# A six-layer cross network on one core: the first 512 rows of the input enter as plain rows and are transposed on TensorE, and the first remainder weights enter as 32 rows

## The chip, the core and the metric

The kernel runs on one core of a Trainium2 chip. A core has TensorE (PE in the profile, with its weight loads shown as PEld), VectorE (DVE), ScalarE (ACT), GpSimd (POOL) and SyncE (SP), and 16 DMA engines that all queues share. The metric is the device time of one launch in microseconds (us). Before the change the median of three runs is 131.31 us (131.15 to 131.46).

## The reference

```python
x = x0                                   # 4096 x 416, bf16
for l in range(6):
    x = x0 * (x @ ws[l] + bs[l]) + x     # ws: 6 x 416 x 416, bs: 6 x 416
```

Six cross layers follow each other. Each multiplies all 4096 rows by a 416 x 416 matrix, adds a bias, multiplies by the original input and adds the layer's input.

## The kernel before, in words

For layers 0 to 4 the activations are kept transposed: the 416 features lie on partitions, the 4096 batch rows on the free axis. 416 is three blocks of 128 features and a remainder of 32. The three blocks are the tile `XM[i]` (128 partitions x 3 x 4096); `XM[0]` holds x0, and two more take the layers' outputs in turn. The batch is cut into two halves `s` of four groups `g` of 512 columns. The 32 remainder features of a half's four groups are stacked on 128 partitions in `XR[i]` (group g on partitions 32g to 32g+31). `XRd` is a copy of x0's remainder with its upper and lower 64 partitions exchanged.

**Loads (lines 100 to 121).** `load_x0t(s, g)` (L76) issues a transposing DMA on SP: 512 rows x 384 columns of x0 arrive as three 128 x 512 blocks of `XM[0]`. All eight are on SP's queue, in the order (0,0), (0,1), (0,2), (0,3), (1,0), then `load_xrem1` (L85), then (1,1) to (1,3). Behind them on SP are the weights of layers 1 to 5, x0 as plain rows for the last layer, and its bias. ACT's queue issues layer 0's weights `WM[:,0]` (L72), the biases `bsb` (L102), four loads `xrig` (L81, the remainder columns of half 0 in 64-byte pieces), and `WR[:,0]` (L88): the 32 remainder rows of layer 0's weights, read four times so that they stand on all four 32-partition groups. A planner gives each DMA one of eight completion semaphores in turn, and an issue that reuses a semaphore first waits for that semaphore's earlier DMA: the WR load waits, on ACT, for the first transposing load.

**TensorE's head.** Two fillers of 256 columns and eight of 512 (L135) run on a constant tile. Then `bias_setup` transposes the biases (L143, L145; VectorE copies them, L146 and L147), and a ninth 512-column filler goes where the planner's order puts it.

**`first_layer(s)`** is the part that the change touches. A PSUM tile `ph` holds 128 output features (block m) x two groups (a pair h), and four such tiles fit in PSUM. For half 0 it goes so:

1. `full(m, 0, 0)` for m = 0, 1, 2: three matmuls each (L206, k = 0, 1, 2) on group 0, nine in all;
2. `x0_rem(0)` (L151): four TensorE transposes of `xrig` into `tpr`, then three VectorE copies (L154), one into `XR[0]` and two of 64 partitions into `XRd`;
3. `full(m, 0, 1)`: nine matmuls on group 1;
4. the row stage (`row`, L213): eight matmuls of 32 rows with `WR`, for pair 0 of each block and for pair 1 of block 0. Those on different 32-row groups of the array run side by side;
5. ScalarE evicts each `ph` with the bias (L159), VectorE multiplies by x0 (L160) and adds the input (L161);
6. pair 1: 18 matmuls L206, four row matmuls, 16 of the remainder outputs (L185, L190) into `pr`, and `x0_rem(1)` for half 1 into the other half of `pr`; ScalarE's eviction of `pr` is L165.

Half 1 is the same without step 2. Layers 1 to 4 (L173, L179) then run on TensorE back to back, and the last layer (L319, L325, L346, L347, L336) writes rows out. `WD` (L125) is a block-diagonal copy of 32 columns of `WR` that GpSimd makes.

The order of instructions on each engine comes from the tile planner; `tc.keep_in_program_order` pins a single instruction to its place in the program.

Of the kernel before, what the change touches and what calls it, by code (L numbers as in the profile page):

```python
# [10 lines left out]
ALU = mybir.AluOpType  # L11
BF16 = mybir.dt.bfloat16
FP32 = mybir.dt.float32
# [3 lines left out]
def kernel(  # L17
# [7 lines left out]
    nc = tc.nc  # L25
    B, D = x0.shape
    L = ws.shape[0]
    P = 128
    NK = 3
    R = D - NK * P  # L30
    assert R == 32 and B == 4096 and D == 416 and L >= 2
    NS = 2
    NG = 4
    CW = 512
# [5 lines left out]
    big = ctx.enter_context(tc.tile_pool(name="big", bufs=1))  # L40
    tpool = ctx.enter_context(tc.tile_pool(name="tpool", bufs=6))
    opool = ctx.enter_context(tc.tile_pool(name="opool", bufs=10))
    psum = ctx.enter_context(tc.tile_pool(name="psum", bufs=4, space=bass.MemoryType.PSUM))

    x0_v = x0.rearrange("(bt p) d -> p bt d", p=P)
    out_v = out.rearrange("(bt p) d -> p bt d", p=P)

    ident = const.tile([P, P], BF16)
    dz = const.tile([P, 2], FP32)
    warm = const.tile([P, CW], BF16)  # L50
    ones = const.tile([P, P], BF16)
    WM = const.tile([P, L, NK, D], BF16)
    WR = const.tile([P, L, D], BF16)
# [3 lines left out]
    bM = const.tile([P, NK, L], FP32)  # L57
    bR = const.tile([P, L], FP32)
    X0rows = big.tile([P, NBT, D], BF16)
    XLrows = big.tile([P, NBT, D], BF16)  # L60
    scrR = [big.tile([P, 4, P], BF16, name=f"scrR{s}") for s in range(NS)]
    xrem = big.tile([P, 16, R], BF16)
    xrig = big.tile([P, NS, 4, P], BF16)
    XRd = big.tile([P, NS * CW], BF16)
    XM = [big.tile([P, NK, B], BF16, name=f"XM{i}") for i in range(3)]
    XR = [big.tile([P, NS * CW], BF16, name=f"XR{i}") for i in range(3)]

    def col0(s, g):
        return SW * s + CW * g

    def load_wm(eng, l):
        eng.dma_start(WM[:, l], ws[l, 0:NK * P, :].rearrange("(k p) n -> p k n", p=P))  # L72

    def load_x0t(s, g):
        c0 = col0(s, g)
        nc.sync.dma_start_transpose(out=XM[0][:, :, c0:c0 + CW], in_=x0[c0:c0 + CW, 0:NK * P])  # L76

    def load_xrem0():
        with nc.allow_non_contiguous_dma(reason="64B row segments"):
            for i in range(4):  # L80
                nc.scalar.dma_start(xrig[:, 0, i, :].rearrange("p (g r) -> p g r", g=NG), x0_v[:, i:16:4, NK * P:D])  # L81

    def load_xrem1():
        with nc.allow_non_contiguous_dma(reason="64B row segments"):
            nc.sync.dma_start(xrem[:], x0_v[:, 16:32, NK * P:D])  # L85

    def load_wr0():
        nc.scalar.dma_start(WR[:, 0, :], ws[0:1, NK * P:D, :].broadcast_to([NG, R, D]))  # L88

    def load_wr(eng, g, l0, l1):  # L90
        eng.dma_start(WR[32 * g:32 * g + 32, l0:l1, :], ws[l0:l1, NK * P:D, :].rearrange("l r n -> r l n"))
# [5 lines left out]
    nc.gpsimd.memset(ones[:], 1.0)  # L97
    nc.gpsimd.memset(WD[:], 0.0)

    load_x0t(0, 0)  # L100
    load_wm(nc.scalar, 0)
    nc.scalar.dma_start(bsb[:], bs[:, :])  # L102
    load_x0t(0, 1)
    load_xrem0()
    load_wr0()
    nc.scalar.activation(dz[:, 1:2], dz[:, 0:1], ACT.Identity, bias=dz[:, 0:1], scale=1.0)  # L106
    for g in range(2, NG):
        load_x0t(0, g)
    load_x0t(1, 0)
# [18 lines left out]
    nc.gpsimd.tensor_copy(xrig[:, 1].rearrange("p i (g r) -> p i g r", g=NG), xrem[:].rearrange("p (g i) r -> p i g r", g=NG))  # L128
    fill_wd(1, L)

    wps = psum.tile([P, CW], FP32, tag="ps", name="wps")

    def pe_filler(n, cols):
        for i in range(n):
            nc.tensor.matmul(wps[:, 0:cols], lhsT=warm[:, 0:P], rhs=warm[:, 0:cols], start=True, stop=True)  # L135

    pe_filler(2, 2 * P)
    pe_filler(8, CW)

    def bias_setup():  # L140
        pb = psum.tile([P, 4, 8], BF16, tag="ps", name="pb")
        for m in range(NK):
            nc.tensor.transpose(pb[:, m, 0:L], bsb[0:L, 128 * m:128 * m + 128], ident[0:L, 0:L])  # L143
        for g in range(NG):
            nc.tensor.transpose(pb[32 * g:32 * g + 32, 3, 0:L], bsb[0:L, NK * P:D], ident[0:L, 0:L], tile_position=(0, 32 * g))  # L145
        nc.vector.tensor_copy(bM[:], pb[:, 0:NK, 0:L])  # L146
        nc.vector.tensor_copy(bR[:], pb[:, 3, 0:L])  # L147

    def x0_rem(s, tpr):
        for i in range(4):  # L150
            nc.tensor.transpose(tpr[:, 128 * i:128 * i + 128], xrig[:, s, i, :], ident[:])  # L151
        for dst, src in ((slice(0, P), slice(0, P)), (slice(64, P), slice(0, 64)), (slice(0, 64), slice(64, P))):
            to = XR[0] if dst == src else XRd
            nc.vector.tensor_copy(to[dst, CW * s:CW * s + CW], tpr[src])  # L154

    def ew_main(l, s, m, h, pt, cur, nxt):
        c0 = col0(s, 2 * h)
        t = tpool.tile([P, 2 * CW], BF16, name="t")
        nc.scalar.activation(t[:], pt[:].rearrange("p a b -> p (a b)"), ACT.Identity, bias=bM[:, m, l:l + 1], scale=1.0)  # L159
        nc.vector.tensor_tensor(out=t[:], in0=t[:], in1=XM[0][:, m, c0:c0 + 2 * CW], op=ALU.mult)  # L160
        nc.vector.tensor_tensor(out=nxt[:, m, c0:c0 + 2 * CW], in0=t[:], in1=cur[:, m, c0:c0 + 2 * CW], op=ALU.add)  # L161

    def ew_rem(l, s, pr, curR, nxtR):
        tr = tpool.tile([P, 2 * CW], BF16, name="t")
        nc.scalar.activation(tr[:, 0:CW], pr, ACT.Identity, bias=bR[:, l:l + 1], scale=1.0)  # L165
        nc.vector.tensor_tensor(out=tr[:, 0:CW], in0=tr[:, 0:CW], in1=XR[0][:, CW * s:CW * s + CW], op=ALU.mult)  # L166
        nc.vector.tensor_tensor(out=nxtR[:, CW * s:CW * s + CW], in0=tr[:, 0:CW], in1=curR[:, CW * s:CW * s + CW], op=ALU.add)  # L167
# [15 lines left out]
    def mm_rem(l, s, pr, cur, curR):  # L183
        for g in range(NG):
            nc.tensor.matmul(pr[32 * g:32 * g + 32, :], lhsT=WD[:, l, g, :], rhs=curR[:, CW * s:CW * s + CW],  # L185
                             start=True, stop=False, tile_position=(0, 32 * g))
        for k in range(NK):
            for g in range(NG):
                c0 = col0(s, g)
                nc.tensor.matmul(pr[32 * g:32 * g + 32, :], lhsT=WM[:, l, k, NK * P:D], rhs=cur[:, k, c0:c0 + CW],  # L190
                      start=False, stop=(k == NK - 1), tile_position=(0, 32 * g))
# [8 lines left out]
    def first_layer(s):  # L200
        cur, curR, nxt, nxtR = XM[0], XR[0], XM[1], XR[1]

        def full(pt, m, h, gl, after_row):
            c0 = col0(s, 2 * h + gl)
            for k in range(NK):
                nc.tensor.matmul(pt[:, gl, :], lhsT=WM[:, 0, k, 128 * m:128 * m + 128], rhs=cur[:, k, c0:c0 + CW],  # L206
                                 start=(k == 0 and not after_row), stop=(k == NK - 1 and after_row))

        def row(pt, m, h, opens):
            for gl in range(2):  # L210
                rg = 32 * ((2 * h + gl) ^ (2 if m == 1 else 0))
                src = XRd if m == 1 else curR
                nc.tensor.matmul(pt[:, gl, :], lhsT=WR[rg:rg + 32, 0, 128 * m:128 * m + 128],  # L213
                                 rhs=src[rg:rg + 32, CW * s:CW * s + CW],
                                 start=opens, stop=not opens, tile_position=(rg, 0))

        def ph(m):
            return psum.tile([P, 2, CW], FP32, tag="ps", name=f"ph{m}")

        pa = [ph(m) for m in range(NK)]  # L220
        if s == 0:
            for m in range(NK):
                full(pa[m], m, 0, 0, False)
            tp0 = psum.tile([P, CW], BF16, tag="ps", name="tpr")
            x0_rem(0, tp0[:])
            for m in range(NK):
                full(pa[m], m, 0, 1, False)
        else:
            for m in range(NK):
                for gl in range(2):  # L230
                    full(pa[m], m, 0, gl, False)
        pb = [ph(0)]
        row(pa[0], 0, 0, False)
        row(pb[0], 0, 1, True)
        row(pa[2], 2, 0, False)
        row(pa[1], 1, 0, False)
        for m in range(NK):
            ew_main(0, s, m, 0, pa[m], cur, nxt)
        for m in range(NK):
            if m:  # L240
                pb.append(ph(m))
            for gl in range(2):
                full(pb[m], m, 1, gl, m == 0)
        row(pb[1], 1, 1, False)
        row(pb[2], 2, 1, False)
        pr = psum.tile([P, 2, CW], FP32, tag="ps", name="pr")
        mm_rem(0, s, pr[:, 0, :], cur, curR)
        if s == 0:
            x0_rem(1, pr[:, 1, :].bitcast(BF16)[:, 0:CW])
        for m in range(NK):  # L250
            ew_main(0, s, m, 1, pb[m], cur, nxt)
        ew_rem(0, s, pr[:, 0, :], curR, nxtR)

    bias_setup()
    pe_filler(1, CW)
    for s in range(NS):
        first_layer(s)

# [14 lines left out]
    cur, curR = XM[1], XR[1]  # L273
    for l in range(1, LL):
        nxt, nxtR = XM[1 + (l % 2)], XR[1 + (l % 2)]
# [4 lines left out]
        def finish(t):  # L280
            s, m = t
            for h in range(2):
                ew_main(l, s, m, h, pts[t][h], cur, nxt)
            if feeds_last:
                xl_dmat(s, m, nxt)
# [19 lines left out]
        cur, curR = nxt, nxtR  # L305

    l = LL
# [97 lines left out]
```

## Time and profile before

| what | value |
|---|---|
| median of 3 runs | 131.31 us (131.15 to 131.46) |
| the profiled execution, its own time | 131.51 us |
| its span, first to last instruction | 129.7 us |
| TensorE busy | 123.4 us, 95% of the span |
| VectorE busy | 107.5 us, 83% |
| ScalarE busy | 85.7 us, 66% |
| GpSimd busy | 6.1 us, 5% |
| mean granted TensorE clock | 0.992 |

The span is 1.8 us shorter than the execution's own time; that part lies outside the instructions. In the lists of groups a row gives busy time and the mean duration of one; a matmul's shown duration overlaps the next one's, so TensorE's pace is read from the starts. The chain view follows the work that ended last back to what released it. In the timeline the first number is the start and the second the length of the merged piece, both in us.

### The profile page before, as it was taken

Reading aid. Unit: us, or ns where it says so; the run is one execution under the profiler, and the core shown is the slowest. Engines: PE = TensorE matmul, PEld = TensorE weight load, DVE = VectorE, ACT = ScalarE, POOL = GpSimd, SP = SyncE. Lnnn points to the kernel's source line nnn. Section 1 sums busy time; section 2 is a strip of 40 time slices with the busy share of each in tenths; the row PEclk is TensorE's granted clock in tenths of the full one; section 3 lists DMA queues with packets and bytes.
Section 4 is the critical chain, followed back from the end, with each engine's and each line's share of the span. In section 5 each row is a group of like instructions: output and inputs, shape, how many; then the busy total and the mean of one; then the engine's idle time right before and its main releaser. Section 6 shows DMA issues by size and latency. Waiting matters only on the chain.

```text
span 129.7 us, 3968 instructions
## 1 busy us (share of the span) xinstructions
PE 123.4 (95%) x1690; PEld 55.1 (42%) x1690; DVE 107.5 (83%) x197; ACT 85.7 (66%) x97; POOL 6.1 (5%) x17
## 2 busy tenths in 40 slices
PE   6999999999999999999999999999999999999960
PEld 2333343444444444444444444444444445445430
DVE  1022999999998898999898989898989899888992
ACT  0044865976849486849476849577848896569670
POOL 4002200800000000000000000000000000000000
PEclk9999999999999999999999999999999999999996
DMA  3999999999990000000000000000197989996754
GB/s 91 240 222 226 167 163 269 257 329 333 332 274 7 0 5 3 5 0 5 0 5 0 5 0 5 0 0 5 26 180 163 121 180 199 187 315 195 237 182 137
DMA packets 42185, 16.45 MB, mean 127 GB/s; under 512 B 30894, under 2 KB 42168, under 8 KB 42168
## 3 DMA queue, kind: packets, MB, share of 16 engines
q1 hardware_dynamic: 39368, 15.53, 54.3%
q10 hardware_dynamic: 2800, 0.67, 2.6%
q8 instruction: 13, 0.21, 0.7%
q14 instruction: 4, 0.03, 0.1%
HBM read 6.23 MB, written 3.41 MB: 74 GB/s over the span
## 4 chain that ended last, share of the span: by engine, by line
PE 73%; DVE 11%; DMA 8%; issue 3%; ACT 2%; DVEq 0%; ACTq 0%
PE pt L173 49%; PE py L319 8%; PE pt L179 5%; PE pr L190 4%; DMA WR<-in_ws_dram 4%; DMA XM<-in_x_dram 4%; DVE t L347 3%; PE ph L206 3%; DVE t L160 2%; DVE XM L161 2%; DVE o L336 2%; PE pr L185 2%; PE ph L213 1%; PE py L325 1%; ACT t L159 1%
## 5 line engine op out<-in xcount | busy, mean ns | idle before, releaser
L173 PE MATMUL pt<-XM,WM 128*32 128x512 bf16 x1152 | 65.2, 379 | 0.0
L159 ACT ACTIVATE t<-pt,bM 128x1024 bf16<-128x1024 f32 x48 | 49.6, 1115 | 18.3 <-PE pt L179 18.3
L160 DVE TENSOR_TENSOR t<-t,XM 128x1024 bf16<-128x1024 bf16 x60 | 41.4, 690 | 6.0 <-ACT t L159 6.0
L161 DVE TENSOR_TENSOR XM<-t,XM 128x1024 bf16<-128x1024 bf16 x60 | 41.8, 697 | 3.5
L173 PEld LDWEIGHTS <-WM 128*32 128x32 bf16 x1152 | 29.7, 97 | 33.8 <-issue 5.1
L346 ACT CAST t<-py 128x416 bf16<-128x416 f32 (+1 forms) x23 | 14.8, 642 | 4.8 <-PE py L319 2.1
L319 PE MATMUL py<-WM,XM 128*128 128x416 bf16 x96 | 17.7, 340 | 0.0
L206 PE MATMUL ph<-XM,WM 128*128 128x512 bf16 x72 | 16.5, 379 | 0.2 <-DMA XM<-in_x_dram 0.2
L159 ACT ACTIVATE t<-ph,bM 128x1024 bf16<-128x1024 f32 x12 | 12.5, 1115 | 4.9 <-PE ph L213 4.9
L319 PEld LDWEIGHTS <-XM 128*128 128x128 bf16 x96 | 9.0, 98 | 8.5 <-issue 1.4
L347 DVE TENSOR_TENSOR t<-t,X0rows 128x416 bf16<-128x416 bf16 (+1 forms) x23 | 10.4, 454 | 1.2 <-ACT t L346 1.2
L206 PEld LDWEIGHTS <-WM 128*128 128x128 bf16 x72 | 6.8, 98 | 8.6 <-issue 1.2
L336 DVE TENSOR_TENSOR o<-t,XLrows 128x416 bf16<-128x416 bf16 (+1 forms) x23 | 10.3, 451 | 0.0
L165 ACT ACTIVATE t<-pr,bR 128x512 bf16<-128x512 f32 x10 | 6.4, 684 | 5.0 <-DVE XRd L154 2.9
L190 PE MATMUL pr<-XM,WM 128*32 128x512 bf16 x120 | 8.2, 379 | 0.0
L179 PE MATMUL pt<-XR,WR 32*128 32x512 bf16 x96 | 7.3, 379 | 0.0
L106 ACT ACT_TABLE_LOAD x1 | 1.3, 1283 | 6.4 <-DMA XM<-in_x_dram 6.4
L135 PE MATMUL wps<-warm 128*128 128x512 bf16 (+1 forms) x11 | 4.1, 561 | 1.2 <-DVE warm L94 1.2
L167 DVE TENSOR_TENSOR XR<-t,XR 128x512 bf16<-128x512 bf16 x10 | 4.2, 424 | 0.7
L190 PEld LDWEIGHTS <-WM 128*32 128x32 bf16 x120 | 3.2, 97 | 3.0
L125 POOL COPY WD<-WR 32x32 bf16<-32x32 bf16 (+1 forms) x8 | 3.6, 454 | 16.0 <-DMA WR<-in_ws_dram 15.6
L166 DVE TENSOR_TENSOR t<-t,XR 128x512 bf16<-128x512 bf16 x10 | 4.2, 418 | 0.0
(37 smaller groups left out, 29.6 us busy)
## 6 DMA issues: line engine op xcount, KB each, us to landing
X0rows<-in_x_dram SPq DMA_DIRECT2D x4, 832.0 KB, 11.6
out_dram<-o SPq DMA_DIRECT2D x9, 208.0 KB, 2.6
WM<-in_ws_dram SPq DMA_DIRECT2D x5, 312.0 KB
out_dram<-o SPq DMA_DIRECT2D x13, 104.0 KB, 1.9
WR<-in_ws_dram SPq DMA_DIRECT2D x4, 130.0 KB, 4.2
WM<-in_ws_dram ACTq DMA_DIRECT2D x1, 312.0 KB
XM<-in_x_dram SPq DMA_TRANSPOSE x8, 5.7
xrig<-in_x_dram ACTq DMA_DIRECT2D x4, 32.0 KB, 4.3
```

The costliest lines, as they stand in the source:

```text
L159: nc.scalar.activation(t[:], pt[:].rearrange("p a b -> p (a b)"), ACT.Identity, bias=bM[:, m, l:l + 1], scale=1.0)
L160: nc.vector.tensor_tensor(out=t[:], in0=t[:], in1=XM[0][:, m, c0:c0 + 2 * CW], op=ALU.mult)
L161: nc.vector.tensor_tensor(out=nxt[:, m, c0:c0 + 2 * CW], in0=t[:], in1=cur[:, m, c0:c0 + 2 * CW], op=ALU.add)
L165: nc.scalar.activation(tr[:, 0:CW], pr, ACT.Identity, bias=bR[:, l:l + 1], scale=1.0)
L173: nc.tensor.matmul(pts[g // 2][32 * q:32 * q + 32, g % 2, :], lhsT=WM[:, l, k, 128 * m + 32 * q:128 * m + 32 * q + 32], rhs=cur[:, k, c0:c ...
L179: nc.tensor.matmul(pts[g // 2][:, g % 2, :], lhsT=WR[32 * g:32 * g + 32, l, 128 * m:128 * m + 128], rhs=curR[32 * g:32 * g + 32, CW * s:CW ...
L190: nc.tensor.matmul(pr[32 * g:32 * g + 32, :], lhsT=WM[:, l, k, NK * P:D], rhs=cur[:, k, c0:c0 + CW], start=False, stop=(k == NK - 1), tile ...
L206: nc.tensor.matmul(pt[:, gl, :], lhsT=WM[:, 0, k, 128 * m:128 * m + 128], rhs=cur[:, k, c0:c0 + CW], start=(k == 0 and not after_row), sto ...
L319: nc.tensor.matmul(py[:, 0:D], lhsT=cur[:, k, q_cols(q, g)], rhs=WM[:, l, k, :], start=((not closes) and k == 0), stop=(closes and k == NK ...
L336: tc.keep_in_program_order(nc.vector.tensor_tensor(out=o, in0=t, in1=xl, op=ALU.add))
L346: nc.scalar.copy(tv, src)
L347: tc.keep_in_program_order(nc.vector.tensor_tensor(out=tv, in0=tv, in1=X0rows[:, b, :], op=ALU.mult))
```

## The change

- The first transposing load is replaced by two plain loads on SP, `xg0[0]` and `xg0[1]`, of 256 whole rows each (128 partitions x 2 x 416). They stand ahead of the other transposing loads on SP.
- TensorE's head becomes: the two short fillers, five of 512 columns in place of eight, six transposes of `xg0[0]` into the PSUM tile `tg0`, two 512-column fillers, six transposes of `xg0[1]`, and the bias transposes, as the program states it. In the planner's order the two fillers stand ahead of all twelve transposes, so seven 512-column fillers follow each other. The ninth filler is gone. VectorE copies `tg0` into `XM[0]` in three copies of 128 x 512.
- Group 0's remainder columns are copied by GpSimd out of `xg0` (two small copies); the four `xrig` loads bring three groups in place of four.
- `WR[:,0]` is loaded as 32 rows, on SP behind the second group's transposing load; ScalarE copies it to two more 32-partition groups and GpSimd to the last.
- In half 0's first step the matmuls of blocks 0 and 1 run k by k, then block 2. `x0_rem(0)` now comes after the group-1 matmuls of blocks 0 and 1.
- The VectorE products of half 0's second pair are kept in program order, which puts the copies of `x0_rem(1)` ahead of them.

```diff
+    xg0 = [big.tile([P, 2, D], BF16, name=f"xg0{a}") for a in range(2)]
...
-                nc.scalar.dma_start(xrig[:, 0, i, :].rearrange("p (g r) -> p g r", g=NG), x0_v[:, i:16:4, NK * P:D])
+                nc.scalar.dma_start(xrig[:, 0, i, R:P].rearrange("p (g r) -> p g r", g=NG - 1),
+                                    x0_v[:, i + 4:16:4, NK * P:D])
...
-        nc.scalar.dma_start(WR[:, 0, :], ws[0:1, NK * P:D, :].broadcast_to([NG, R, D]))
+        nc.sync.dma_start(WR[0:R, 0, :], ws[0, NK * P:D, :])
...
-    load_x0t(0, 0)
+    for a in range(2):
+        nc.sync.dma_start(xg0[a][:], x0_v[:, 2 * a:2 * a + 2, :])
...
+    for a in range(2):
+        nc.gpsimd.tensor_copy(xrig[:, 0, 2 * a:2 * a + 2, 0:R], xg0[a][:, :, NK * P:D])
+    for g in range(1, NG):
+        dst, src = WR[32 * g:32 * g + 32, 0, :], WR[0:R, 0, :]
+        if g < NG - 1:
+            nc.scalar.copy(dst, src)
+        else:
+            nc.gpsimd.tensor_copy(dst, src)
...
-    wps = psum.tile([P, CW], FP32, tag="ps", name="wps")
+    wps = psum.tile([P, 2, CW], FP32, tag="ps", name="wps")
+    tg0 = psum.tile([P, NK, CW], BF16, tag="ps", name="tg0")
+    pb = wps[:, 1, :].bitcast(BF16)[:, 0:32].rearrange("p (m l) -> p m l", m=4)
...
+    def g0_transposes(a):
+        for k in range(NK):
+            for i in range(2):
+                c = 128 * (2 * a + i)
+                nc.tensor.transpose(tg0[:, k, c:c + 128], xg0[a][:, i, 128 * k:128 * k + 128], ident[:])
...
-    pe_filler(2, 2 * P)
-    pe_filler(8, CW)
+    pe_filler(2, 2 * P)
+    pe_filler(5, CW)
+    g0_transposes(0)
+    pe_filler(2, CW)
+    g0_transposes(1)
+    bias_transposes()
+    for k in range(NK):
+        nc.vector.tensor_copy(XM[0][:, k, 0:CW], tg0[:, k, :])
+    nc.vector.tensor_copy(bM[:], pb[:, 0:NK, 0:L])
+    nc.vector.tensor_copy(bR[:], pb[:, 3, 0:L])
...
-        nc.vector.tensor_tensor(out=t[:], in0=t[:], in1=XM[0][:, m, c0:c0 + 2 * CW], op=ALU.mult)
+        prod = nc.vector.tensor_tensor(out=t[:], in0=t[:], in1=XM[0][:, m, c0:c0 + 2 * CW], op=ALU.mult)
+        if pin:
+            tc.keep_in_program_order(prod)
...
-            for m in range(NK):
-                full(pa[m], m, 0, 0, False)
+            for k in range(NK):
+                for m in range(NK - 1):
+                    full(pa[m], m, 0, 0, False, (k,))
+            full(pa[NK - 1], NK - 1, 0, 0, False)
             tp0 = psum.tile([P, CW], BF16, tag="ps", name="tpr")
-            x0_rem(0, tp0[:])
             for m in range(NK):
                 full(pa[m], m, 0, 1, False)
+                if m == 1:
+                    x0_rem(0, tp0[:])
...
-            ew_main(0, s, m, 1, pb[m], cur, nxt)
+            ew_main(0, s, m, 1, pb[m], cur, nxt, pin=(s == 0))
...
-    bias_setup()
-    pe_filler(1, CW)
```

More of the change, by code (lines that the diff above doesn't have):

```diff
@@ L129, with bias_transposes @@
     fill_wd(1, L)
-    wps = psum.tile([P, CW], FP32, tag="ps", name="wps")
+    wps = psum.tile([P, 2, CW], FP32, tag="ps", name="wps")
+    tg0 = psum.tile([P, NK, CW], BF16, tag="ps", name="tg0")
+    pb = wps[:, 1, :].bitcast(BF16)[:, 0:32].rearrange("p (m l) -> p m l", m=4)
     def pe_filler(n, cols):
         for i in range(n):
-            nc.tensor.matmul(wps[:, 0:cols], lhsT=warm[:, 0:P], rhs=warm[:, 0:cols], start=True, stop=True)
-    pe_filler(2, 2 * P)
-    pe_filler(8, CW)
-    def bias_setup():
-        pb = psum.tile([P, 4, 8], BF16, tag="ps", name="pb")
+            nc.tensor.matmul(wps[:, 0, 0:cols], lhsT=warm[:, 0:P], rhs=warm[:, 0:cols], start=True, stop=True)
+    def g0_transposes(a):
[3 more added lines that the diff above has]
+                nc.tensor.transpose(tg0[:, k, c:c + 128], xg0[a][:, i, 128 * k:128 * k + 128], ident[:])
+    def bias_transposes():
         for m in range(NK):
@@ L145, in bias_setup @@
             nc.tensor.transpose(pb[32 * g:32 * g + 32, 3, 0:L], bsb[0:L, NK * P:D], ident[0:L, 0:L], tile_position=(0, 32 * g))
-        nc.vector.tensor_copy(bM[:], pb[:, 0:NK, 0:L])
-        nc.vector.tensor_copy(bR[:], pb[:, 3, 0:L])
+    pe_filler(2, 2 * P)
[8 more added lines that the diff above has]
+    nc.vector.tensor_copy(bR[:], pb[:, 3, 0:L])
     def x0_rem(s, tpr):
@@ L154, in x0_rem, with ew_main @@
             nc.vector.tensor_copy(to[dst, CW * s:CW * s + CW], tpr[src])
-    def ew_main(l, s, m, h, pt, cur, nxt):
+    def ew_main(l, s, m, h, pt, cur, nxt, pin=False):
         c0 = col0(s, 2 * h)
@@ L201, in first_layer, with full @@
         cur, curR, nxt, nxtR = XM[0], XR[0], XM[1], XR[1]
-        def full(pt, m, h, gl, after_row):
+        def full(pt, m, h, gl, after_row, ks=range(NK)):
             c0 = col0(s, 2 * h + gl)
-            for k in range(NK):
+            for k in ks:
                 nc.tensor.matmul(pt[:, gl, :], lhsT=WM[:, 0, k, 128 * m:128 * m + 128], rhs=cur[:, k, c0:c0 + CW],
```

## The prediction

> **What bounds the kernel now.** I read the page first (busy shares, then the chain), then the chain of the first 32 us in order of time, then the timelines of TensorE, ScalarE and VectorE over the same stretch, and last a table of the first microseconds. TensorE is busy 95% of the span, and from about 27.5 us it goes through layers 1 to 4 with no wait above a tenth of a microsecond. So the change is worth what it moves the start of layer 1 (L173).
>
> The chain of the first 32 us, start and length:
>
> ```profile
> 0.74 5.01 DMA XM<-in_x_dram
> ...
> 5.76 5.23 DMA WR<-in_ws_dram
> ...
> 11.47 1.12 ACT t L159
> ...
> 20.56 0.44 DVE XRd L154
> ...
> 21.08 0.70 ACT t L165
> ...
> 21.82 0.60 PE ph L213 x6
> 22.42 3.99 PE ph L206 x18
> ```
>
> The first transposing load lands at 5.75; it also releases the issue of the WR load on ACT's queue, which lands at 10.99. Later the chain goes through VectorE's copies of half 1's remainder (L154) and the eviction L165 that waits for them.
>
> TensorE's timeline over the same stretch:
>
> ```profile
> 5.79 2.10 PE L206 MATMUL ph<-XM,WM 128*128 128x512 bf16 x9 [0.19 <-DMA XM<-in_x_dram]
> 7.72 0.22 PE L151 MATMUL tpr<-ident,xrig 128*128 128x128 bf16 x1
> 8.14 0.70 PE L151 MATMUL tpr<-ident,xrig 128*128 128x128 bf16 x3 [0.20 <-DMA xrig<-in_x_dram]
> 8.83 2.10 PE L206 MATMUL ph<-XM,WM 128*128 128x512 bf16 x9
> 11.04 0.60 PE L213 MATMUL ph<-XR,WR 32*128 32x512 bf16 x6
> 11.28 0.38 PE L213 MATMUL ph<-XRd,WR 32*128 32x512 bf16 x2
> 11.59 4.15 PE L206 MATMUL ph<-XM,WM 128*128 128x512 bf16 x18
> ...
> 16.97 0.40 PE L151 MATMUL pr<-ident,xrig 128*128 128x128 bf16 x4
> 17.20 4.05 PE L206 MATMUL ph<-XM,WM 128*128 128x512 bf16 x18
> 21.19 0.39 PE L213 MATMUL ph<-XR,WR 32*128 32x512 bf16 x2
> 21.82 0.40 PE L213 MATMUL ph<-XR,WR 32*128 32x512 bf16 x4 [0.24 <-ACT t L165]
> ```
>
> Three waits are seen: for xrig and the second group (7.95 to 8.83), for WR (10.78 to 11.04), and in half 1's row stage, which takes 1.16 us from 21.19 to the next L206 at 22.35, where the same stage at 11.04 took 0.55. A 512-column matmul costs 0.215 ((2.10 - 0.38)/8), a transpose in a run 0.06 plus a tail of 0.22 (the row at 16.97).
>
> Weight loads of the fillers show their pace; each 512-column filler takes 0.43 until 4.58, twice the later 0.215:
>
> ```profile
> 3.72 0.15 PEld L135 LDWEIGHTS <-warm 128*128 128x128 bf16 x1 [0.28 <-issue]
> 4.15 0.15 PEld L135 LDWEIGHTS <-warm 128*128 128x128 bf16 x1 [0.28 <-issue]
> 4.58 0.15 PEld L135 LDWEIGHTS <-warm 128*128 128x128 bf16 x1 [0.28 <-issue]
> ```
>
> **The change part by part.** Call F the start of the first real matmul; before, F = 5.79.
>
> Loads up to F. The planner puts seven 512-column fillers together, so TensorE is free for the transposes at 4.58 (the row above; before, it went on with fillers). When are the rows there? SP issues the two loads from 0.74, some 0.46 each (ACT's issue of 312 KB takes that), beside ACT's WM. Ahead of or beside the last of them are 312 + 5 + 416 KB = 750 kB. The table of the first microseconds has 17 GB/s in 1 to 2, 200 in 2 to 3, 253 and 267 in the next two: 217 kB by 3.0, and the other 533 take 2.0 us at those rates, or 1.6 at the 339 that 21 to 22 us shows. So the second load lands at 4.6 to 5.0, with some 0.1 for the completion 4.7 to 5.1; I take 4.95. The first (half the sum) is there near 3.9, under the fillers. Below 4.7 nothing is gained, since TensorE is the later; above 5.1 every microsecond counts in full.
>
> Transposes: six from 4.58, of which three at half pace (0.12) until about 4.9 and the rest at 0.06, to about 5.1; six more, 0.30 + 0.22, to 5.63. Then VectorE's first copy of 128 x 512, 0.42 by the row of L154's copies, with 0.04 on either side: F = 6.15. The other two copies run beside two matmuls each (0.43 for 0.46). The seven bias transposes (0.27 before) lie under that copy. First term: 6.15 - 5.79 = +0.36.
>
> From F to pair 1's matmuls. Group 0's nine matmuls take 1.98, with the copies' pace. Group 1 must be there at F + 1.98 = 8.13. Before, it landed 3.05 after the first load (5.75 to 8.8), with 128 KB of xrig in 64-byte pieces beside it; now it starts behind the plain loads with 96 KB of xrig, so at the latest 4.95 + 3.05 = 8.0: no wait, with 0.1 to spare by this bound. Six matmuls (1.29), four transposes (0.24), then VectorE's three copies 0.42 + 0.46 + 0.43 end at F + 5.03. TensorE has done its last three group-1 matmuls and the row matmuls of blocks 0 and 2 by F + 4.7 and waits for the slot and data of those copies; the last four rows follow in two steps, since they need the same 32-row groups, and L206 goes on at F + 5.61. Before it was 11.59 - 5.79 = 5.80. Second term: -0.19. A wait on XRd has taken the place of the wait on WR.
>
> WR. Its issue on SP waits for WM's semaphore (landed near 4.5), so what stands behind it on SP, the loads of groups 2 and 3, is issued near 5.0 where it was 4.92. WR's 26 KB land behind group 1, near 8.4. Two ScalarE copies of 32 x 416 (at most 0.64 each, the 128 x 416 row) and one on GpSimd (0.20 for 32 x 32 to 2.1 when 0.81 for 32 x 160 is scaled up) end by 10.5; the rows need the last at F + 5.07 = 11.2. Cost nothing, under a cover of 0.7. The table load on ACT moves to about 4.5, long before the first eviction.
>
> Group 3. Its landing delays one L206 now: 18 in 4.15 against 4.06 elsewhere. It is issued as early, behind less, and needed 0.2 later: third term -0.09 (0 at worst).
>
> Half 1's row stage. With the products kept in order, VectorE does x0_rem(1)'s copies after three pairs of L160 and L161 rather than five. TensorE's transposes for it come near 17.2, so the copies end near 18.6 instead of 20.98; L165 follows and frees its PSUM slot at 19.3, and TensorE needs it near 21. The stage falls to 0.55: fourth term -0.61. VectorE idles about 1 us before these copies, then holds two pairs more; it ends half 1 some 0.6 later than the 31.85 of before, and its reader, the remainder matmuls of half 1 in layer 1, comes at 34: covered by 1.5.
>
> GpSimd now copies beside VectorE's XR and XRd copies (9.8 to 11.2). Beside a GpSimd copy of 0.93 one L161 took 0.98 in place of 0.69, so 0 to +0.3; I take +0.1, since the copies there are short.
>
> Sum: 0.36 - 0.19 - 0.09 - 0.61 + 0.10 = -0.43. The profiled execution took 131.51 (129.7 in the span, 1.8 around it), which gives 131.08. The median of the runs is 0.20 below it, so I state 130.9.
>
> **The rivals.** Differences within 0.2% (0.26 us) can't be told from none.
>
> The plain rows come late. Three streams share the 16 engines, and the slice 1 to 2 us moved only 17 GB/s: if x0's first rows start as slowly as WM's did, half a microsecond is added. The second load landing 0.3 to 0.6 after 5.1 takes most of the gain: about 131.3. For it: the slow start is in the table. Against: 5.1 already takes the low rates.
>
> Group 1 comes late. Slower from its landing at about 8.8, as it is now, on: that is 0.7 of wait, a total of 131.55, and 132.0 at 9.2. For it: group 1's interval of 3.05 was long though nothing else was large, so what follows it may hold it. Against: less is ahead of it.
>
> The half pace lasts. If twelve transposes in place of two fillers hold off the doubling near 4.9, the half pace goes on until as much full work is done again: 3.7 us from the first filler to the doubling, so until about 8.3. The transposes then cost 0.6 more, and 1.5 us of matmuls are done at half pace, 0.8 lost: 132.3. Against: the fillers are the same until 4.58, 90% of the time to the doubling, and four transposes at 16.97 run at full pace between matmuls. The Trainium skill, "TensorE: Matmul & The Clock Gate", section "Part 4: PE-mode transpose", says that transposes don't count as TensorE work for this clock in the usual way; by that rule this case is what happens if the window is judged on its last third of a microsecond. The row of transposes at 16.97 shows only that a short run doesn't lower the pace; no run here shows whether one holds off the rise.
>
> The copies to XR are hidden after all, or the rows come at 4.7: at best F is 6.06 and the GpSimd cost 0: 130.7.
>
> **How the numbers follow.** My sum, with its own range of 130.65 to 131.05: 0.58. Rows late, no change: 0.20. Group 1 late (0.14) and half pace (0.06), slower: 0.20. A last 0.02 is for what I haven't seen, slower. The likeliest gives 130.9. The low end is the best sum less 0.1 for the scatter of the runs, 130.6; leaving out the half pace and the far end of group 1's lateness, the high end is 131.8.
>
> **What would show it.** Right: L206 starts near 6.15 after copies of tg0; no DMA wait before group 1's L206; a wait of about 0.4 on VectorE within the row stage at 10.8; L206 near 11.75; L165 near 19 and half 1's row stage in 0.55; L173 from 27.1. Wrong: fillers or matmuls spaced 0.43 after 5; the transposes waiting for xg beyond 5.1; group 1 landing after 8.3; WR rows waiting for ACT or POOL; or L173's start moved without the end of the span moving with it.

## The result, and the profile after

The changed kernel takes 131.68 us (median of 22 executions, 131.34 to 133.63); the kernel before, on the same chip, takes 131.30 (22 executions, 131.07 to 131.59). The ratio is 1.0031, 95% interval 1.0020 to 1.0043: slower by some 0.4 us, where 130.9 and faster was forecast. The ratio leaves out executions more than 1.5% above a kernel's fastest, which here are four at 133.4 to 133.6; since the experiments below bear on them, the raw list matters: sixteen executions lie between 131.34 and 131.81, two at 132.5, four at 133.4 to 133.6.

The profiled execution took 131.49 (span 129.7). It is one of the faster ones of its kernel, while before's 131.51 was one of the slower of its own. So the two traces differ by 0.02 where the usual executions differ by 0.4, and part of the answer has to come from other runs.

The chain of the first 28 us in order of time (start, length, what):

```profile
1.25 4.21 DMA xg<-in_x_dram
...
6.53 3.40 PE ph L232 x15
...
11.08 0.43 DVE XRd L178
...
11.65 0.60 PE ph L239 x4
```

The chain has one load in it, the second plain row load; then it is TensorE but for one wait, on VectorE's copies of the remainder. The load of WR and the eviction L165, both links of the chain before, are gone from it.

TensorE's timeline of the same kernel (start and length in us; in brackets the idle time ahead of the piece and what ended it):

```profile
4.29 0.50 PE L154 MATMUL tg<-ident,xg 128*128 128x128 bf16 x6
5.51 0.51 PE L154 MATMUL tg<-ident,xg 128*128 128x128 bf16 x6 [0.72 <-DMA xg<-in_x_dram]
...
6.53 3.40 PE L232 MATMUL ph<-XM,WM 128*128 128x512 bf16 x15 [0.24 <-DVE XM L169]
...
10.73 0.60 PE L239 MATMUL ph<-XR,WR 32*128 32x512 bf16 x4
11.65 0.39 PE L239 MATMUL ph<-XR,WR 32*128 32x512 bf16 x2 [0.32 <-DVE XRd L178]
...
12.19 4.06 PE L232 MATMUL ph<-XM,WM 128*128 128x512 bf16 x18
...
21.70 0.60 PE L239 MATMUL ph<-XR,WR 32*128 32x512 bf16 x6
...
22.24 4.06 PE L232 MATMUL ph<-XM,WM 128*128 128x512 bf16 x18
...
27.43 0.82 PE L199 MATMUL pt<-XM,WM 128*32 128x512 bf16 x12
```

Three things are to be seen. TensorE stands idle for 0.72 until the second row load lands, and F, the start of the first real matmul, is 6.53. From F on nothing waits for a load: fifteen L232 follow each other, the second group being there. Half 1's row stage, from 21.70 to 22.24, takes 0.54. Layer 1 (L199) starts at 27.43, where it started at 27.54. From there to the end both executions take 104.0 to 104.1 (131.51 - 27.54 and 131.49 - 27.43), so in these two traces the head is all there is to explain.

### The profile page after: what moved, and what is told of

Same layout as the page of the kernel before. It is cut to its first block, busy times and chain, and to the rows that moved or that the text cites. A ratio compares the mean times of both kernels' runs of the same rounds, so it can differ in the third digit from the quotient of the medians.

```text
span 129.7 us, 4000 instructions
## 1 busy us (share of the span) xinstructions
PE 122.8 (95%) x1700; PEld 55.5 (43%) x1700; DVE 108.1 (83%) x200; ACT 86.9 (67%) x99; POOL 6.5 (5%) x20
## 4 chain that ended last, share of the span: by engine, by line
PE 84%; DVE 6%; DMA 3%; issue 2%; ACT 1%; SPq 0%; DVEq 0%
PE pt L199 49%; PE ph L232 12%; PE py L346 8%; PE pt L205 5%; PE pr L216 5%; DVE t L374 3%; DMA xg<-in_x_dram 3%; DVE o L363 2%; PE pr L211 2%; PE ph L239 1%; PE py L352 1%; PE py L355 1%; ACT t L373 1%; DVE XRd L178 1%; PE tg L154 0%
## 5 line engine op out<-in xcount | busy, mean ns | idle before, releaser
L199 PE MATMUL pt<-XM,WM 128*32 128x512 bf16 x1152 | 65.2, 379 | 0.0
L199 PEld LDWEIGHTS <-WM 128*32 128x32 bf16 x1152 | 29.7, 97 | 33.8 <-issue 5.1
L232 PE MATMUL ph<-XM,WM 128*128 128x512 bf16 x72 | 16.4, 379 | 0.2 <-DVE XM L169 0.2
L232 PEld LDWEIGHTS <-WM 128*128 128x128 bf16 x72 | 6.8, 98 | 8.4 <-issue 1.1
L191 ACT ACTIVATE t<-pr,bR 128x512 bf16<-128x512 f32 x10 | 6.4, 684 | 2.7 <-PE pr L216 2.1
L169 DVE COPY XM<-tg 128x512 bf16<-128x512 bf16 x3 | 1.1, 417 | 4.6 <-PE tg L154 4.6
L148 PE MATMUL wps<-warm 128*128 128x512 bf16 (+1 forms) x9 | 3.3, 543 | 1.2 <-DVE warm L96 1.2
## 6 DMA issues: line engine op xcount, KB each, us to landing
out_dram<-o SPq DMA_DIRECT2D x13, 104.0 KB, 1.7
```

The lines of the kernel that those rows point to most:

```text
L199: nc.tensor.matmul(pts[g // 2][32 * q:32 * q + 32, g % 2, :], lhsT=WM[:, l, k, 128 * m + 32 * q:128 * m + 32 * q + 32], rhs=cur[:, k, c0:c ...
```

## The experiments

After the first runs I held two theories of the 0.4 us. One: the second row load is late, and nothing else. The other: the point at which TensorE's pace doubles is not fixed, and the new head is open to a late doubling, where the old one was not. The first three experiments take the change apart; the next ones test the two theories; the last looks for a better kernel.

**e1: the order of VectorE's products alone.** The kernel before, with the products of half 0's second pair kept in program order.

```diff
-            ew_main(0, s, m, 1, pb[m], cur, nxt)
+            ew_main(0, s, m, 1, pb[m], cur, nxt, pin=(s == 0))
```

> The kernel before with one part of the change alone: half 0's pair-1 products kept in program order. Theory A (the fourth term of the prediction): half 1's row stage falls from 1.16 to about 0.55 us and nothing gives it back, so the time falls by 0.5 to 0.6, from 131.3 to about 130.7. Rival B (VectorE's idle time before the moved copies comes back later): within 0.2 of 131.3.

Measured: 130.98 (12 executions, 130.89 to 131.31), ratio 0.9980 (0.9972 to 0.9989). Its TensorE timeline:

```profile
5.85 2.60 PE L208 MATMUL ph<-XM,WM 128*128 128x512 bf16 x9
...
8.77 2.10 PE L208 MATMUL ph<-XM,WM 128*128 128x512 bf16 x9
...
21.13 0.60 PE L215 MATMUL ph<-XR,WR 32*128 32x512 bf16 x6
...
21.67 4.06 PE L208 MATMUL ph<-XM,WM 128*128 128x512 bf16 x18
```

The row stage falls to 0.54 as worked out, and the kernel gains, but 0.26 to 0.35 us instead of 0.6. The first piece holds more: nine matmuls took 2.60 instead of 2.10, because the pace doubled only at 6.9 in this execution. It cost nothing. The second group is waited for until 8.77 anyway.

**e3: that, and WR as 32 rows.** The transposing load of the first group stays.

```diff
-        nc.scalar.dma_start(WR[:, 0, :], ws[0:1, NK * P:D, :].broadcast_to([NG, R, D]))
+        nc.sync.dma_start(WR[0:R, 0, :], ws[0, NK * P:D, :])
...
+    for g in range(1, NG):
+        dst, src = WR[32 * g:32 * g + 32, 0, :], WR[0:R, 0, :]
+        if g < NG - 1:
+            nc.scalar.copy(dst, src)
+        else:
+            nc.gpsimd.tensor_copy(dst, src)
```

> The kernel before with the kept order and WR as 32 rows on SP, copied by ScalarE and GpSimd, but with group 0 still by the transposing load: the change without its plain rows. Theory A (the plain rows are what costs): WR no longer ends the row stage's wait, which starts at 10.8 in place of 11.04; 130.3 to 130.6, the best of all. Rival B (the 32 rows and their copies cost as much as the four-fold load): no better than the kept order alone, 130.7 or above.

Measured: 130.87 (12 executions, 130.62 to 131.38), ratio 0.9976 (0.9963 to 0.9989). This beats both kernels, though it can't be told from e1, so the second forecast held: WR as 32 rows adds nothing that shows. In e1's trace the row stage starts at 10.83 with the four-fold load, so the wait for WR until 11.04 is not in every execution. Two lines of its TensorE timeline:

```profile
11.43 4.20 PE L214 MATMUL ph<-XM,WM 128*128 128x512 bf16 x18
...
26.81 1.47 PE L181 MATMUL pt<-XM,WM 128*32 128x512 bf16 x24
```

The changed kernel differs from e3 by the row loads and what goes with them in the head (the transposes, the copies, the place of `x0_rem(0)`). It reaches the matmuls of pair 1 at 12.19 where e3 has 11.43, and layer 1 at 27.43 where e3 has 26.81: 0.62 in the traces, and 1.0031 - 0.9976 = 0.55% or 0.7 us in the usual executions. So the row loads lose what the other two parts win, and more.

**e2: the changed kernel without the pinned order.**

```diff
-            ew_main(0, s, m, 1, pb[m], cur, nxt, pin=(s == 0))
+            ew_main(0, s, m, 1, pb[m], cur, nxt)
```

> The changed kernel without that order. Theory A: its usual time of 131.5 to 131.8 rises by about 0.5, to 132.0 to 132.3, and half 1's row stage shows 1.1 us again. Rival B: no change, 131.5 to 131.8.

Measured: 131.89 (6 executions, 131.63 to 132.46), ratio 1.0058 (1.0038 to 1.0079), which overlaps the changed kernel's interval. From its ScalarE timeline:

```profile
20.80 0.69 ACT L191 ACTIVATE t<-pr,bR 128x512 bf16<-128x512 f32 x1 [2.12 <-DVE XRd L178]
```

The row stage runs from 21.65 to 22.19, so it takes 0.54 without the pin too. The eviction L191 ends at 21.49, 0.16 before the rows need its slot; with the pin it starts at 19.32 and there are 1.7 us to spare. So in this trace the new head alone makes the stage short, by coming later to it, and the pin adds margin.

**e5: WM's load behind the row loads.** Tests the first theory: the second row load shares the DMA engines with WM's 312 KB.

```diff
-    load_wm(nc.scalar, 0)
+    load_wm(nc.sync, 0)
```

> The changed kernel with layer 0's weights WM loaded on SP behind the two row loads in place of on ACT beside them. Theory A (the second row load lands 0.4 to 0.5 us later than predicted because WM's load shares the engines with it): it lands by 4.3 and no longer holds TensorE, the first real matmul comes at 6.0 to 6.5 (by where the pace doubles), TensorE's idle time before the last transposes is gone, and the long executions get fewer; 131.2 to 131.5. Rival B (the rows are slow by themselves): it lands after 5.0 as now, 131.5 to 131.8; with WM later by as much, slower still.

Measured: 131.47 (11 executions, 131.21 to 131.85), ratio 1.0012 (1.0001 to 1.0022). GpSimd copies the remainder columns of each row load as soon as it lands, so its timeline tells the landings. The copy after the second load, first in the changed kernel and then in e5:

```profile
5.51 0.24 POOL L111 COPY xrig<-xg 128x64 bf16<-128x64 bf16 x1 [1.08 <-DMA xg<-in_x_dram]
```

```profile
4.17 0.24 POOL L111 COPY xrig<-xg 128x64 bf16<-128x64 bf16 x1 [0.45 <-DMA xg<-in_x_dram]
```

And e5's TensorE timeline:

```profile
6.10 3.41 PE L232 MATMUL ph<-XM,WM 128*128 128x512 bf16 x15 [0.33 <-DMA WM<-in_ws_dram]
...
27.01 1.25 PE L199 MATMUL pt<-XM,WM 128*32 128x512 bf16 x20
```

The second load lands 1.3 earlier, the twelve transposes follow each other without a gap from 4.57 on, and F falls from 6.53 to 6.10; now it waits for WM. So sharing with WM costs this load 1.3 us, and without it layer 1 starts 0.42 earlier. (The prediction's sum had counted WM's bytes, so this alone is not why its landing was wrong; that is answered below.) None of the eleven executions is above 131.9, where the changed kernel has seven of 31 (with e6) at 132.4 or above; eleven are too few to say that the long ones are gone.

**e6: the changed kernel once more,** for a second trace.

> The changed kernel as it is, for a second trace beside the others on one chip. Theory C: usual executions 131.4 to 131.9 and some of 132.4 to 133.6; where the fillers' pace doubles later than the 3.99 us of the first trace, the last transposes and with them the first real matmul come later by up to 0.4. Rival D: the pace doubles at the same time in every execution, and only the landing of the second row load moves the first matmul.

Measured: 131.58 (9 executions, 131.51 to 132.62), ratio 1.0037 (1.0020 to 1.0054). Its TensorE timeline:

```profile
4.57 1.34 PE L154 MATMUL tg<-ident,xg 128*128 128x128 bf16 x12
...
6.43 3.40 PE L232 MATMUL ph<-XM,WM 128*128 128x512 bf16 x15 [0.25 <-DVE XM L169]
```

The same kernel as the trace above, but the first six transposes are 0.107 apart, not 0.056: this time the pace doubled at 5.3, where it had doubled at 4.0. The second load landed at 5.4 again, so term 1 is not a chance event. The later doubling did not make the first real matmul later here, as the first forecast allowed: it starts at 6.43, since the last transposes had to wait for the load anyway.

**e7: transposes in place of fillers.** The kernel before, with 34 transposes instead of its nine 512-column fillers, to see whether transposes hold the doubling off.

```diff
-    pe_filler(8, CW)
+    pe_transposes(34)
...
-    pe_filler(1, CW)
```

> The kernel before with its nine 512-column fillers replaced by 34 transposes of the constant tile, back to back. If transposes count as work for the pace like matmuls: the pace doubles before 7.4 as in the other traces, the transposes are spaced 0.11 until then, and the time is 131.1 to 131.6. If they don't: transposes and the first matmuls stay at half pace until about 3 to 6 us after the first real matmul at 5.8, and the time rises by 0.7 to 2.5 us, to 132.0 to 133.8.

Measured: 131.55 (11 executions, 131.26 to 131.68), ratio 1.0019 (1.0010 to 1.0027). Its TensorE timeline:

```profile
1.59 3.83 PE L140 MATMUL wps<-ident,warm 128*128 128x128 bf16 x34
...
5.75 2.24 PE L211 MATMUL ph<-XM,WM 128*128 128x512 bf16 x9
```

With hardly any work but transposes up to 5.4, the nine real matmuls take 2.24 against 2.10: the pace doubled during the first of them, at 6.1. If transposes did not count, it would have had to wait for work that began at 5.75. The Trainium skill, "TensorE: Matmul & The Clock Gate", section "Part 4: PE-mode transpose", says that the fast clock doesn't engage for transposes because they don't count as busy in the same way. This trace disagrees, and so does the changed kernel's, whose transposes run 0.056 apart once the pace has doubled. The profile names these instructions MATMUL and does not show whether they run in the mode that the section means. A wait of 0.55 for a later group's load (until 18.51) may be why this kernel is a little slower than before; what made that load late I have not tried.

**e8 and e12: idle time alone.** The kernel before with two, and with six, of its nine 512-column fillers left out; nothing else is changed. e8 is shown; e12 has 3 in place of 7.

```diff
-    pe_filler(8, CW)
+    pe_filler(7, CW)
...
-    pe_filler(1, CW)
```

> The kernel before with seven fillers of 512 columns in place of nine, so that TensorE idles for about 0.9 us before the first real matmul at 5.8, as it does in the changed kernel before its last transposes, but without added transposes. If the idle time alone makes the pace double late: some executions, about one in four, 0.7 to 2 us longer than 131.3. If the idle time does not matter: all within 131.0 to 131.6.

> The kernel before with three filler matmuls of 512 columns instead of nine and nothing else changed: TensorE idles from about 3 us to the first real matmul at about 5.8, and there is no transpose of x0 in the head. Theory (idle time in the warm-up is enough to put the pace's doubling off): the first group's matmuls are about 0.43 us apart until 8 or later, the wait for the second group (until 8.8) hides part of that, and the time is 131.8 to 133.0, with no or few executions at the 131.2 of before. Rival (the late doublings come from the transposes or from the plain row loads, idle time is harmless): the matmuls are 0.43 us apart only until 5 to 7, the second group is waited for as before, and the time is 131.2 to 131.5.

Measured, e8: 131.85, ratio 1.0044 (1.0019 to 1.0069), in two groups of six: 131.10 to 131.55 and 132.15 to 132.56. Its trace is of the first group (131.30). Measured, e12: 132.18 (7 executions, 131.70 to 133.29), ratio 1.0090 (1.0056 to 1.0123). The TensorE timeline of e12's execution of 132.18:

```profile
5.75 3.72 PE L206 MATMUL ph<-XM,WM 128*128 128x512 bf16 x9 [0.70 <-DMA XM<-in_x_dram]
...
9.53 2.11 PE L206 MATMUL ph<-XM,WM 128*128 128x512 bf16 x9
```

Nine matmuls take 3.72: their starts are 0.43 apart until 8.7, and the pace doubles only at 9.1. The wait for the second group, which lasted until 8.83 before, hides all but 0.70 of the 1.62 lost. No transpose of x0 and no row load is in this head, so idle time is enough. e8's slower half fits the same cause, with the same size, but none of it was traced.

**e9: the changed kernel with three 512-column fillers instead of seven.**

```diff
-    pe_filler(5, CW)
+    pe_filler(3, CW)
     g0_transposes(0)
-    pe_filler(2, CW)
     g0_transposes(1)
```

> The changed kernel with three of the filler matmuls of 512 columns instead of seven, so that TensorE idles longer ahead of the first real matmul. Theory (the pace doubles at a time of its own in each execution, and where TensorE has idled or works lightly just then it is put off by about 3.4 us of work): most executions now miss the early doubling; the trace shows the first group's matmuls about 0.43 us apart well into the eighteen, layer 1 starts later than the changed kernel's 27.43 by 1 us or more, and the median is 132.5 to 134. Rival (fillers only have to fill the time, any doubling comes by 5 us): the loads set the first real matmul as before, 6.4 to 6.6, and the time is the changed kernel's 131.5 to 131.7.

Measured: 133.70 (5 executions, 133.22 to 134.42), ratio 1.0209 (1.0186 to 1.0232). Its TensorE timeline:

```profile
6.90 4.75 PE L231 MATMUL ph<-XM,WM 128*128 128x512 bf16 x15 [0.23 <-DVE XM L168]
...
29.14 2.76 PE L198 MATMUL pt<-XM,WM 128*32 128x512 bf16 x48
```

The transposes at half pace (0.82 for the last six in place of 0.51), and a landing 0.06 later, make F 0.37 later, and the fifteen matmuls take 4.75 instead of 3.40, with the doubling at 9.7. Here nothing hides it: 0.37 + 1.35 = 1.72, and layer 1 starts 1.71 later. The same delay costs the changed head all of what it costs the old one in part.

**e10 and e4: the gap filled.** In e10 the changed kernel's fillers and transposes are held in their written order: five fillers, six transposes, two fillers, six transposes. In e4 it is seven fillers, six transposes, four fillers, six transposes. e10's edit, of which e4 has the same and the other counts:

```diff
-            nc.tensor.matmul(wps[:, 0, 0:cols], lhsT=warm[:, 0:P], rhs=warm[:, 0:cols], start=True, stop=True)
+            tc.keep_in_program_order(nc.tensor.matmul(wps[:, 0, 0:cols], lhsT=warm[:, 0:P], rhs=warm[:, 0:cols], start=True, stop=True))
...
-                nc.tensor.transpose(tg0[:, k, c:c + 128], xg0[a][:, i, 128 * k:128 * k + 128], ident[:])
+                tc.keep_in_program_order(nc.tensor.transpose(tg0[:, k, c:c + 128], xg0[a][:, i, 128 * k:128 * k + 128], ident[:]))
```

> The changed kernel with its fillers and transposes held in the order in which they are written: five fillers, the first row load's six transposes, two fillers, the second's six. Fillers now lie inside the gap that the changed kernel has between its two sets of transposes. Theory (it is the gap in TensorE's work that puts the doubling off in some executions): no execution near 132.5 or 133.5, median 131.4 to 131.8. Rival (the late landing of the second row load is all that costs): as the changed kernel, 131.6, with a spread up to 133.6.

> The changed kernel with the fillers kept in program order: seven before the first six transposes, four (about 0.9 us) between them and the last six, so that TensorE hardly idles before 5.5. Theory C (the idle 0.9 us and the transposes let the half pace last in some executions, which gives the executions of 132.5 to 133.6): no execution above 132.0, the others as the changed kernel, 131.4 to 131.8. Rival D (the long executions come from loads that land late): executions above 132.4 as often as in the changed kernel, about one in four.

Measured, e10: 131.75 (9 executions, 131.36 to 132.29), ratio 1.0041 (1.0027 to 1.0055). Measured, e4: 132.32 (6 executions, 131.90 to 132.91), ratio 1.0090 (1.0068 to 1.0112). e10's TensorE timeline:

```profile
4.75 1.06 PE L148 MATMUL wps<-warm 128*128 128x512 bf16 x2
...
6.97 3.40 PE L232 MATMUL ph<-XM,WM 128*128 128x512 bf16 x15 [0.23 <-DVE XM L169]
```

e10's theory held: nothing above 132.29, a median of 131.75. e4's did not: it allowed nothing above 132.0, and five of its six executions lie above that, three of them above 132.4. Neither has an execution at 133.4 or above, but the changed kernel has only four of 31 there, so fifteen without one say little: that filling the gap takes the long executions away is not shown. It gains nothing either way. In e4's trace the fillers hold the last transposes until 6.21, well after the load has landed, and F is 7.23. In e10's they end at 5.61, 0.1 after the landing would have let the transposes go, but the pace is still halved, the last six transposes take 0.85 in place of 0.51, and F is 6.97.

**e11: e5, with the remainder of the first group formed early.** In place of after the fifteenth matmul, `x0_rem(0)` comes right after group 0's nine, as in the kernel before.

```diff
-    load_wm(nc.scalar, 0)
+    load_wm(nc.sync, 0)
...
+            x0_rem(0, tp0[:])
             for m in range(NK):
                 full(pa[m], m, 0, 1, False)
-                if m == 1:
-                    x0_rem(0, tp0[:])
```

> The changed kernel with WM's load behind the two row loads on the same ring, and the remainder of x0's first group formed right after group 0's products, as in the kernel before, instead of after the fifteenth matmul. Theory (the head's costs are the second row load's landing beside WM's and the 0.3 to 0.9 us wait for XRd's copies at the remainder rows): the wait for XRd goes, layer 1 starts 0.5 to 0.7 us before the 27.01 of the kernel with WM's load behind alone, at 26.3 to 26.6, and the time is 130.5 to 130.9. Rival (something else ends last, group 1 or a wait at half 1): layer 1 starts at 26.9 or later and the time stays at 131.2 to 131.5.

Measured: 131.25 (12 executions, 130.83 to 132.19), ratio 1.0006 (0.9990 to 1.0022). Its TensorE timeline:

```profile
11.89 3.40 PE L232 MATMUL ph<-XM,WM 128*128 128x512 bf16 x15 [0.19 <-DMA XM<-in_x_dram]
...
17.82 3.40 PE L232 MATMUL ph<-XM,WM 128*128 128x512 bf16 x15 [0.25 <-DMA XM<-in_x_dram]
```

The wait for XRd's copies is gone, and two waits for later transposing loads have taken its place; layer 1 starts at 26.89, and of e5's 27.01 only 0.12 is won. The rival was right here: once the head is quick, the stream of transposing loads sets the start of layer 1 near 26.9, which e1 and e3 reach without the row loads.

## Why the prediction was wrong

By its own steps, in the profiled execution:

| step | predicted | measured | where |
|---|---|---|---|
| loads up to F | +0.36 | +0.74 | F 6.53 in place of 6.15 |
| F to pair 1's matmuls | -0.19 | -0.14 | 12.19 - 6.53 = 5.66, against 5.80 |
| group 3 | -0.09 | -0.09 | 18 in 4.06 |
| half 1's row stage | -0.61 | -0.62 | 0.54 against 1.16 |
| GpSimd beside VectorE's copies | +0.10 | 0 | L178's copies at 0.42 and 0.43 |
| start of layer 1 | -0.43 | -0.11 | 27.43 against 27.54 |

With 0.09 more from there to the end, the profiled execution came out 0.41 above the 131.08 of the sum, and 0.38 of that is the first term.

**The step that failed: "Loads up to F", in its term for the completion.** It put the second load's landing at 4.95, and no later than 5.1: the bytes moved by 4.6 to 5.0, and 0.1 more for the completion. It landed at 5.46, and at 5.4 to 5.5 in the five other traces with WM's load beside the rows (e2, e4, e6, e9, e10). The bytes were not late. The changed kernel's stretches (first to last microsecond and length, then busy time of the engines, the granted clock, the DMA share and GB/s):

```profile
1.00:2.00 1.00, 0.81 (x3) 0.43 (x4) 0.41 (x3) 0.00 (x0) 0.92 (x3) 1.00 0.12 25
2.00:3.00 1.00, 1.00 (x4) 0.43 (x3) 0.00 (x0) 0.00 (x0) 0.12 (x1) 1.00 0.86 240
3.00:4.00 1.00, 1.00 (x4) 0.32 (x3) 0.00 (x0) 0.00 (x0) 0.00 (x0) 1.00 1.01 324
4.00:5.00 1.00, 0.79 (x8) 0.42 (x6) 0.00 (x0) 0.43 (x1) 0.24 (x1) 1.00 1.32 263
```

25 + 240 + 324 is 589 kB by 4.0, and at 263 the 750 kB that I had counted have moved by 4.6. The packets say when the rows were through. The two row loads, WM and the biases move in packets of one row, 832 bytes: 512 + 384 + 6 = 902 of them. The other loads of that time move in packets under 512 bytes. The packets that start from 0 to 4.85, and those that start from 4.85 to 5.46:

```profile
DMA packets 1517, 0.83 MB, mean 171 GB/s; under 512 B 615, under 2 KB 1517, under 8 KB 1517
```

```profile
DMA packets 526, 0.10 MB, mean 172 GB/s; under 512 B 526, under 2 KB 526, under 8 KB 526
```

In the first stretch 1517 - 615 = 902 packets are of whole rows, so all of them had started by 4.85, with some 80 kB of later loads among them (0.83 MB against 750 kB). In the second stretch there is none. From the last row to the landing it took 0.6 us, where the sum has 0.1. No run here shows 0.1 for this load: in the other five traces the last row packet starts at 4.8 to 4.9, and the load lands 0.55 to 0.67 later. With 0.6 the same sum gives 5.45. What fills this time stays open. Later loads were moving in it (0.10 MB), and whether it is shorter without them I have not tried.

So the rival "the plain rows come late" had the size, 0.3 to 0.6 after 5.1, which I gave 0.20, but not the reason: the rows did not start slowly, and their bytes came when the sum had them.

**A second assumption in the same step:** that the pace doubles near 4.9, since it did in the trace of before. It doubles at another time in each execution, 1.3 us apart in the two traces of the changed kernel itself (4.0, and 5.3 in e6). In the traces of heads with work up to about 4.3 or longer, the spacing halved at 4.0 (the changed kernel and e3), 4.4, 4.8, 4.9, 5.3, 5.5, 6.1 and 6.9 us, and between 6.2 and 7.0 in e10; with three fillers at 9.1 and 9.7. The rival "the half pace lasts" had the right place and a wrong reason: it blamed the transposes (e7: they count) and was priced at 0.06 because most of the work ahead of the doubling was unchanged. Idle time before F puts the doubling off (e12, e9), though it also came at 6.1 and 6.9 in heads with hardly any (e7, e1). In the old head the wait for the second group hides a late doubling (e1's 6.9, at no cost), while the new head from F on waits for no load. The four executions at 133.4 to 133.6 and the two at 132.5 fit this. A doubling late by x after F costs x/2 here, so 2 us more means a doubling some 4 us after F by this estimate; e9's came 2.8 after. But no long execution of the changed kernel itself was traced, so for it the cause is inferred from e9 and e12, not shown.

**The half-1 row stage.** The size was right in the trace. In the old head the pin makes it (e1); in the new one the stage takes 0.54 without the pin too (e2), so there the figure came out right partly by luck, without the step that I gave for it. And the usual execution of before gains only 0.26 to 0.35 from the pin (e1). I had taken the waits of one execution, itself 0.2 above the median, for waits of the kernel, and may so have taken the 0.2 off twice, here and for the median; no trace of a usual execution of before shows it. In e1's trace layer 1 starts 0.68 earlier than in that of before, and 0.2 of it is lost again between there and the end (131.03 - 26.86 = 104.17). Without the pin, traces of the old head show this stage at 1.02 (e8) to 1.39 (e12), and at 0.54 in e7, which comes to it late after a wait; so why the usual gain is smaller stays open.

**The median.** 130.9 was forecast and 131.68 measured. By my estimate, about 0.4 of the 0.78 is the landing and about 0.3 the smaller gain from the pin (0.61 less 0.26 to 0.35); the last 0.1 I can't assign.

**What held.** WR's wait went, and a wait on XRd's copies stands in its place (TensorE goes on with L239 at 11.65, where those at 10.73 were the last that it could do). The second group was there in time, so the rival "group 1 comes late" did not occur. The copies of WR were hidden. One term held by its cover and not by its step: the loads of groups 2 and 3 were not issued near 5.0 but from 5.48, just after the second row load had landed, and group 3's matmuls still did not wait for them.

## What to carry to other kernels

Before a load is replaced by a quicker one at the head of a kernel, add up what shares the engines with it until its last byte, and add the time from the last byte to the landing as a trace of the kernel shows it (0.6 us here, not 0.1). The row loads here did not pay even with WM's load out of their way (e5, e11), because the next loads then set the time. A wait that looks like a loss can be the slack that absorbs something that varies from one execution to the next: where a head is tightened, look at several executions, and do not take out fillers before TensorE's pace has doubled without timing it (e8, e9 and e12 lost by it). The cheap part of a change is worth timing alone: here the order of VectorE's products, with or without the smaller load of WR, gives 0.2% to 0.24%, and the costly part took more than that back.

## What the runs showed of the hardware that I had not expected

The time at which TensorE's pace doubles ranged over 2.9 us (4.0 to 6.9) in heads whose work began at 1.19 every time and went on without a long gap; the kernel before, e1 and e3 have the same fillers, and theirs doubled at 4.9, 6.9 and 4.0. The Trainium skill, "TensorE: Matmul & The Clock Gate", section "What's actually happening", says that the clock is judged over a free-running window of about 3.4 us, and so changes at a time that differs from run to run, by half a microsecond either way. The traces agree that it differs and show a wider spread. No run here shows the window itself.

The granted clock of the profile does not show this half pace. In e9, where matmuls start 0.43 apart until 9.7, the stretch from 7.5 to 8.5 (columns as above; the number ahead of the DMA share is the granted clock) reads:

```profile
7.50:8.50 1.00, 1.00 (x3) 0.29 (x2) 0.16 (x3) 0.02 (x1) 0.00 (x0) 1.00 1.23 248
```

It says 1.00, though its three matmuls lie at half the pace of those after 9.7. The pace has to be read from the starts.

A row load's last packet and its landing lay 0.55 to 0.67 us apart in six traces, as told above.
